# A planned one-core kernel: new port rules, prices and constants in the planner that orders its instructions

## The chip, the cores and the metric

The kernel runs on one core of a Trainium2 chip. The metric is device time of one execution in microseconds (us): the median over the runs. The names of the engines are those of the profile: PE multiplies matrices, DVE (VectorE) does elementwise work and reductions along a row, ACT (ScalarE) does copies, exponentials and gelu, POOL (GpSimd) does reductions across partitions here and nothing else, SP issues nearly all transfers. About 0.2% of the time (2.1 us) is what a measurement of this kernel can tell from no change.

## The reference

```python
def phi(x):
    proj = np.einsum('bhsd,df->bhsf', x, w_phi)
    proj = proj - np.max(np.abs(proj), axis=-1, keepdims=True)
    return np.concatenate([np.exp(proj), np.exp(-proj)], axis=-1)
q_p, k_p = (phi(q), phi(k))
kv = np.einsum('bhsf,bhsd->bhfd', k_p, v)
z = np.sum(k_p, axis=2)
num = np.einsum('bhsf,bhfd->bhsd', q_p, kv)
den = np.einsum('bhsf,bhf->bhs', q_p, z)[..., None] + 1e-06
attn = num / den                     # 8 batches, 8 heads, 576 tokens, 64
...
x = attn.transpose(0, 2, 1, 3).reshape(4608, 512)
h = x @ w_in                         # 512 x 2048
g = 0.5 * h * (1.0 + erf(h / sqrt(2)))
return g @ w_out                     # 2048 x 512
```

So eight batches of a linear attention with 128 features of both signs, and then a two-layer perceptron over all 4608 tokens. A token's row of x is whole only when all eight heads of its batch are done.

## The kernel before, in words

The attention goes batch by batch. For k: `pk` (PE, keys times features, in a PSUM tile "pp" that has one buffer and is shared with `pq`), `mx` (DVE, largest absolute value along the row, L435), the subtraction into `ek` or, for the rest of the keys, `er` (DVE, L371), two exponentials (ACT, L440), and `kv` (PE), copied out as `kvn`. The last two parts of a name such as `ek_1_1_1_1` say batch, half of the heads, pair in it and sign; only in batch 0 every second `pk` has another bank. For q: `pq` (PE), its copy `pc` (ACT, L365), `mb` (POOL, absolute maximum over the partitions, L501, one buffer), the subtraction `pc<-pc,mb` (DVE, L371), two exponentials `ef` (ACT), and `pn` (PE, one PSUM bank), copied out as `xo` (ACT) and stored to `x_d`. Of batches 0 and 1 the denominator is a row of `pn` (65 rows); from batch 2 on DVE makes `un` from `ef` (L530, L533) and POOL adds it over the partitions as `db` (L536). The quotients come from `d_d` by `dc` (L556, L557) and go to `r_d`.

The weights come as 32 pieces in 64-bit floats: `raw`, then `wt` by ACT (L386) and by four DVE steps (L387, L389 with one input, L391, L393 with two), then a high part (ACT, L365) and a low part (DVE, L371): `w_i` and `w_o`.

The perceptron goes in 18 blocks of 256 tokens. `tokens` (L588 on) loads `xr` and the quotients into `xh`, multiplies, and splits into `xh` and `xl` (all on DVE). `up` writes `ph` (24 matmuls for two columns of 128 features), then gelu into `gh` and `gl`, then `po`. Blocks 0 to 7 run beside the attention of batches 1 to 7 and the later weights. Blocks 8 to 17 use a product with seven instead of eight multiplications (`pa`, `pb`, with sums of weights `tw` that are stored as `t_d` and fetched when the attention's memory is given back).

Nothing of the order is written by hand. Every operation is given to `Plan.op` (L81) with its engine, a cost in us, and a rank. `Plan.order` (L109) is a list scheduler: for each engine it works out when each operation whose inputs are there could start (`start_of`, L128), takes the one that starts first, among equals the one of lowest rank, and moves that engine's clock. Between engines it adds `HOP` (L63); for a change of shape on PE `BEHIND` and `BEFORE` (L67, L68). `READS` (L70) is how long DVE is held at the start of a POOL reduction; `port` says which DVE operations are held. Ranks come from the constants at the end of the file: T0, LEAD, AT, HOLD and ATR for attention, T0, WR and WSPAN for weights, T0, T15 and T18 for the blocks, SUMSAT and SUMSEACH for the sums of weights. `emit` (L245) then issues all operations in the planned order, and each engine runs its own instructions in that order.

## Time and profile before

| what | value |
| --- | --- |
| median of 3 runs (lowest to highest) | 1070.29 us (1070.09 to 1070.43) |
| the profiled execution's own time | 1070.03 us |
| span in the trace, first to last instruction | 1068.3 us |
| mean granted clock of PE | 0.991 |
| busy: PE, DVE, ACT, POOL | 1037.0, 694.7, 625.8, 329.8 us |

Busy time is the sum of the stretches in which the engine works. "Idle before, releaser" in a row is the time that the engine stood still ahead of that instruction and what ended the wait. [...]

### The profile page before, as it was taken

How to read it: one execution, taken by the hardware profiler on the slowest of the kernel's cores; microseconds unless marked ns; L12 is line 12 of the kernel's file. 1: busy time of each engine (PE TensorE's matmuls, PEld its weight loads, DVE VectorE, ACT ScalarE, POOL GpSimd, SP SyncE). 2: the span in 40 equal slices, each digit the busy share in tenths (PEclk: the TensorE clock that was granted, in tenths of full speed). 3: DMA queues.
4: the chain of work that ended last, by engine and by line, in shares of the span. 5: the costliest groups of instructions: out<-in, count | busy, mean ns of one | idle time of the engine just before them, and what ended most of it. 6: DMA issues, size and time to landing. Idle time of an engine off the chain costs nothing.

```text
span 1068.3 us, 24224 instructions
## 1 busy us (share of the span) xinstructions
PE 1037.0 (97%) x9858; PEld 908.0 (85%) x9858; DVE 694.7 (65%) x1303; ACT 625.8 (59%) x1073; POOL 329.8 (31%) x116
## 2 busy tenths in 40 slices
...
GB/s 245 201 223 204 210 122 141 103 104 166 131 100 148 123 111 141 134 76 100 60 64 55 49 200 268 21 60 44 17 60 41 21 60 41 21 60 41 2 21 21
DMA packets 87392, 107.11 MB, mean 100 GB/s; under 512 B 25120, under 2 KB 68288, under 8 KB 87280
## 3 DMA queue, kind: packets, MB, share of 16 engines
...
q8 instruction: 77, 1.26, 0.5%
...
q10 hardware_dynamic: 144, 0.26, 0.1%
...
## 4 chain that ended last, share of the span: by engine, by line
PE 78%; DVE 10%; ACT 5%; issue 3%; DMA 3%; POOL 1%; SPq 0%; DVEq 0%; ACTq 0%; POOLq 0%
PE ph L330 32%; PE po L330 13%; PE pa L330 10%; PE pb L330 8%; PE pn L330 5%; PE kv L330 4%; PE pq L330 3%; PE pk L330 2%; DVE mx L435 1%; DVE ek L371 1%; DVE ts L371 1%; ACT ek L440 1%; DMA dc<-d_d 1%; POOL db L536 1%; DVE w_i L371 1%
## 5 line engine op out<-in xcount | busy, mean ns | idle before, releaser
L330 PE MATMUL ph<-xh,w_i 128*128 128x256 f32 x2304 | 411.9, 277 | 0.6 <-DVE gl L371 0.3
L330 PEld LDWEIGHTS ph<-xh,w_i 128*128 128x128 f32 x2304 | 355.1, 188 | 3.9 <-issue 2.4
L330 PE MATMUL ph<-xl,w_i 128*128 128x256 f32 x1152 | 318.3, 276 | 0.0
L536 POOL PARTITION_ALL_REDUCE db<-un x48 | 182.6, 3804 | 144.5 <-DVE un L533 133.0
L330 PEld LDWEIGHTS ph<-xl,w_i 128*128 128x128 f32 x1152 | 216.3, 188 | 0.3
L501 POOL PARTITION_ALL_REDUCE mb<-pc x64 | 149.5, 2337 | 148.5 <-ACT pc L365 106.0
L371 DVE TENSOR_TENSOR sg<-ga 128x256 f32<-128x256 f32 (+1 forms) x240 | 84.6, 375 | 149.8 <-ACT ga L710 149.0
L330 PE MATMUL po<-w_o,gh 128*128 128x512 f32 (+1 forms) x519 | 164.7, 400 | 0.0
L710 ACT ACTIVATE ga<-ph 128x512 f32<-128x512 f32 x80 | 47.8, 598 | 158.3 <-PE ph L330 156.6
L330 PEld LDWEIGHTS po<-w_o,gh 128*128 128x128 f32 x519 | 93.1, 188 | 28.5 <-issue 6.3
L330 PE MATMUL pa<-w_o,oh 128*128 128x256 f32 x640 | 112.8, 276 | 0.0
L330 PE MATMUL pn<-ef,kvn 128*64 128x288 f32 (+1 forms) x512 | 95.4, 419 | 6.5 <-ACT xo L365 6.4
L330 PE MATMUL po<-w_o,gl 128*128 128x512 f32 (+1 forms) x291 | 101.1, 367 | 0.1
L507 ACT ACTIVATE ef<-pc 128x576 f32<-128x576 f32 x128 | 81.8, 678 | 25.2 <-DVE pc L371 24.4
L330 PEld LDWEIGHTS pa<-w_o,oh 128*128 128x128 f32 x640 | 96.4, 188 | 0.0
L371 DVE TENSOR_TENSOR gl<-ph,gh 128x512 fp32r<-128x512 f32 x64 | 43.9, 688 | 73.9 <-ACT ph L633 70.2
L330 PE MATMUL pa<-w_o,ol 128*128 128x256 f32 x320 | 88.3, 276 | 0.0
L330 PE MATMUL pb<-tw,uh 128*128 128x256 f32 x480 | 85.6, 276 | 0.0
L440 ACT ACTIVATE ek<-ek 128x1024 f32<-128x1024 f32 x64 | 67.8, 1059 | 23.9 <-DVE ek L371 23.2
L530 DVE TENSOR_SCALAR un<-ef,kvn 128x288 f32<-128x288 f32 x96 | 53.3, 576 | 31.3 <-POOL db L536 23.5
L330 PEld LDWEIGHTS pb<-tw,uh 128*128 128x128 f32 x480 | 72.3, 188 | 0.0
L330 PEld LDWEIGHTS pn<-ef,kvn 128*64 128x64 f32 (+1 forms) x512 | 38.5, 136 | 38.0 <-ACT xo L365 14.0
...
## 6 DMA issues: line engine op xcount, KB each, us to landing
...
```

Source lines behind the costliest of these rows:

```text
L330: return tc.keep_in_program_order(nc.tensor.matmul(*a, **kw))
L371: op(eng, cost, lambda: e.tensor_tensor(out=dst(), in0=a(), in1=b(), op=o), r=r, w=w, **kw)
L435: op("dve", dve(256 * n, True), lambda: nc.vector.tensor_reduce(out=mx(), in_=xs(), axis=AX.X, op=ALU.max, apply_absolute_value=True), r=[ ...
L440: op("act", act(256 * n), lambda s=s: nc.scalar.activation(e[s](), e[1](), AF.Exp, scale=1.0 - 2.0 * s), r=[e[1]], w=[e[s]], table="exp", ...
L501: op("pool", 2.28, lambda mb=mb, pc=pc: nc.gpsimd.partition_all_reduce(mb(), pc(), P, bass_isa.ReduceOp.absmax), r=[pc], w=[mb], port="max ...
L507: op("act", act(2 * HS), lambda ef=ef, pc=pc, s=s: nc.scalar.activation(ef()[:, s], pc(), AF.Exp, scale=1.0 - 2.0 * s), r=[pc], w=[ef], ta ...
L530: op("dve", dve(HS, fast=True) + 0.06, lambda un=un, ef=ef, one=one, j=j: nc.vector.tensor_scalar(out=un()[:, j], in0=ef()[:, 0, j], scala ...
L536: op("pool", 3.8, lambda db=db, un=un: nc.gpsimd.partition_all_reduce(db(), un(), P, bass_isa.ReduceOp.add), r=[un], w=[db], port="add", * ...
L710: op("act", act(2 * TB, True) + 0.037, lambda ph=ph, ga=ga: nc.scalar.activation(ga(), ph(), AF.Gelu), r=[ph_all], w=[ga], table="gelu", a ...
```

## The change

Only the planner and its inputs change; each operation does what it did, and some `po` pairs that were emitted in two halves are emitted whole. Lines of the kernel after are 8 or 9 higher.

- `port` becomes a number: 1 for DVE operations with two inputs in SBUF, 2 for those with one (the memset, the first two steps of `wt`, the first step of `un`, the sum in `dc`, the cast to `xh`), 0 for those that read PSUM and for the reciprocal.
- A POOL reduction may start in the plan as soon as its input is there; its end is still counted from when DVE has finished (`port[0]`). The 0.45 us behind every POOL operation is gone.
- DVE is held in two windows: for `READS` from the start (port 1 and 2), and in a later window `WRITES` (port 2 alone).
- Leaving an `f` matmul (`ph`, `po`) for another shape is priced 0.09 us higher (`turn`), what PE waits for 0.07 us later (`PESLACK`), a quotient load at three times its bytes, the reductions at 2.14 and 3.59 us for 2.28 and 3.8.
- The constants were set anew.

```diff
-    READS = {"max": 1.12, "add": 2.38, "sum": 1.27}
+    READS = {"max": 1.15, "add": 2.45, "max main": 2.1, "add main": 4.43, "max rest": 1.05, "add rest": 2.15}
+    WRITES = {"max": (1.4, 2.02), "add": (2.75, 3.47), "max main": (2.3, 3.42), "add main": (4.6, 5.97), "max rest": (1.2, 1.83), "add rest": (2.4, 3.1)}
...
+    def turn(self, a, b):
+        return self.BEHIND[a] + self.BEFORE[b] + (0.09 if a == "f" and b != "d" else 0.0)
...
-        o.port = port if port is not None else eng == "dve"
+        o.port = port if port is not None else int(eng == "dve")
...
-            if o.eng == "pool" and o.port:
-                t = max(t, port[0])
...
-            if o.eng == "dve" and o.port and port[1] <= t < port[2]:
-                t = port[2]
+            if o.eng == "dve":
+                for a, z, least in port[1:]:
+                    if o.port >= least and a <= t < z:
+                        t = z
...
-                if best is None or key[1] < best[1]:
+                if best is None or key[1] < best[1] or key[1] == best[1] and e == "pool":
...
-            o.start, o.end = t, run(t, cost, o.duty) if o.eng == "pe" else t + cost
+            o.start = t
+            if o.eng == "pool" and o.port:
+                t = max(t, port[0])
+                a, z = self.WRITES[o.port]
+                port[1:] = [(t, t + self.READS[o.port], 1), (t + a, t + z, 2)]
+            o.end = run(t, cost, o.duty) if o.eng == "pe" else t + cost
...
-            clock[o.eng] = o.end + (0.45 if o.eng == "pool" else 0.0)
+            clock[o.eng] = o.end
...
-                    slot_free_at[b.tag][b.slot] = o.end + o.late + self.HOP[o.eng]
+                    slot_free_at[b.tag][b.slot] = o.end + o.late + self.HOP[o.eng] + (PESLACK if b.tag in self.banks else 0.0)
...
-            op("pool", 2.28, lambda mb=mb, pc=pc: nc.gpsimd.partition_all_reduce(
+            op("pool", 2.14, lambda mb=mb, pc=pc: nc.gpsimd.partition_all_reduce(
...
-                   r=[r_d[b][h]], w=[xh_all], kb=n * 1.024, rank=rank(0) - 8)
+                   r=[r_d[b][h]], w=[xh_all], kb=n * 3.0, rank=rank(0) - 8)
...
-WSPAN = 36.41
+WSPAN = 48.61
...
-LEAD = 217.42
+LEAD = 333.47
...
-T0 = 95.44
+T0 = 121.19
```

What DVE does at the very beginning: in the rows, `pc` is the query side of batch 0 and `mx`, `ek` its key side, `wt_i0_0` the first piece of the first weight. Before:

```order
L371 TENSOR_TENSOR pc_0_0_0_141<-pc_0_0_0_141,mb_0_0_0_145 128x576
L371 TENSOR_TENSOR er_0_1_166<-pk_0_r_156,mx_0_r_161 128x512
L435 TENSOR_REDUCE mx_0_0_0_196<-pk_0_0_0_173 128x8
L371 TENSOR_TENSOR pc_0_1_0_150<-pc_0_1_0_150,mb_0_1_0_170 128x576
L371 TENSOR_TENSOR ek_0_0_0_1_205<-pk_0_0_0_173,mx_0_0_0_196 128x1024
L435 TENSOR_REDUCE mx_0_0_1_210<-pk_0_0_1_185 128x8
L387 TENSOR_SCALAR wt_i0_0_194<-wt_i0_0_194 128x512
```

and after:

```order
L379 TENSOR_TENSOR pc_0_0_0_141<-pc_0_0_0_141,mb_0_0_0_145 128x576
L379 TENSOR_TENSOR er_0_1_168<-pk_0_r_156,mx_0_r_161 128x512
L395 TENSOR_SCALAR wt_i0_0_166<-wt_i0_0_166 128x512
L397 TENSOR_SCALAR wt_i0_0_166<-wt_i0_0_166 128x512
L399 SCALAR_TENSOR_TENSOR wt_i0_0_166<-raw_i0_0_128,wt_i0_0_166 128x512
L379 TENSOR_TENSOR pc_0_1_0_150<-pc_0_1_0_150,mb_0_1_0_170 128x576
L443 TENSOR_REDUCE mx_0_0_0_204<-pk_0_0_0_174 128x8
L443 TENSOR_REDUCE mx_0_0_1_211<-pk_0_0_1_191 128x8
L379 TENSOR_TENSOR ek_0_0_0_1_213<-pk_0_0_0_174,mx_0_0_0_204 128x1024
L379 TENSOR_TENSOR ek_0_0_1_1_215<-pk_0_0_1_191,mx_0_0_1_211 128x1024
```

Three steps of the first weight and one subtraction of queries now stand between `er_0_1` and the first `mx` of whole tiles, where before `mx_0_0_0` came directly.

DVE around the last `ek` of batch 1 (`ek_1_1_1_1`), whose matmuls `kv_1_1_1` stand shortly ahead of the first `ph` on PE; `wt_o4`, `wt_o5` are pieces of the second matrix, `xr_0` is the first block's tokens. Before:

```order
L435 TENSOR_REDUCE mx_1_1_1_959<-pk_1_1_1_903 128x8
L371 TENSOR_TENSOR pc_1_0_0_878<-pc_1_0_0_878,mb_1_0_0_899 128x576
L371 TENSOR_TENSOR w_i1_1_957<-wt_i1_1_838,w_i1_1_957 128x512
L371 TENSOR_TENSOR w_i2_1_963<-wt_i2_1_848,w_i2_1_963 128x512
L371 TENSOR_TENSOR ek_1_1_1_1_979<-pk_1_1_1_903,mx_1_1_1_959 128x1024
L387 TENSOR_SCALAR wt_i3_1_984<-wt_i3_1_984 128x512
L371 TENSOR_TENSOR xr_0_540<-xr_0_540,xh_0_859 128x1024
L389 TENSOR_SCALAR wt_i3_1_984<-wt_i3_1_984 128x512
```

and after:

```order
L379 TENSOR_TENSOR pc_1_1_0_911<-pc_1_1_0_911,mb_1_1_0_934 128x576
L395 TENSOR_SCALAR wt_o4_936<-wt_o4_936 128x512
L395 TENSOR_SCALAR wt_o5_945<-wt_o5_945 128x512
L397 TENSOR_SCALAR wt_o4_936<-wt_o4_936 128x512
L397 TENSOR_SCALAR wt_o5_945<-wt_o5_945 128x512
L399 SCALAR_TENSOR_TENSOR wt_o4_936<-raw_o4_769,wt_o4_936 128x512
L443 TENSOR_REDUCE mx_1_1_1_977<-pk_1_1_1_950 128x8
L401 SCALAR_TENSOR_TENSOR wt_o4_936<-raw_o4_769,wt_o4_936 128x512
L399 SCALAR_TENSOR_TENSOR wt_o5_945<-raw_o5_852,wt_o5_945 128x512
L379 TENSOR_TENSOR xr_0_481<-xr_0_481,xh_0_781 128x1024
L379 TENSOR_TENSOR w_o4_1030<-wt_o4_936,w_o4_1030 128x512
L379 TENSOR_TENSOR ek_1_1_1_1_1038<-pk_1_1_1_950,mx_1_1_1_977 128x1024
```

The same `ek` now stands behind the token product `xr_0` and behind pieces of `w_o4` and `w_o5` that stood behind it; its row on DVE is 103, and was 87.

PE from the last `kv` of batch 1 to the first matmul of block 0 (`ph_0_0`); the rows of `kv_1_1_1` between are left out. Before:

```order
L330 MATMUL pn_0_3_1_1_999<-ef_0_3_1_856,kvn_0_1_1_524 65x288 x2
L330 MATMUL pk_2_r_1009<-wst_114,kr_2_389 128x128 x4
L330 MATMUL kv_1_1_1_1026<-vt_1_1_844,er_1_0_557 64x65 x2
...
L330 MATMUL kv_1_1_1_1026<-vt_1_1_844,ek_1_1_1_1_979 64x65 x2
L330 MATMUL pn_1_0_0_0_1076<-ef_1_0_0_970,kvn_1_0_0_772 65x288 x2
L330 MATMUL pn_1_0_0_1_1094<-ef_1_0_0_970,kvn_1_0_0_772 65x288 x2
L330 MATMUL pq_1_1_1_1107<-qt_1_1_1_895,wst_114 128x288 x2
L330 MATMUL pq_1_2_0_1126<-qt_1_2_0_1002,wst_114 128x288 x2
L330 MATMUL pn_1_0_1_0_1133<-ef_1_0_1_1019,kvn_1_0_0_772 65x288 x2
L330 MATMUL pk_2_0_0_1144<-wst_114,kt_2_0_713 128x128 x8
L330 MATMUL pn_1_0_1_1_1165<-ef_1_0_1_1019,kvn_1_0_0_772 65x288 x2
L330 MATMUL ph_0_0_1172<-xh_0_859,w_i0_0_287 128x256
```

and after:

```order
L338 MATMUL pn_1_0_0_0_1033<-ef_1_0_0_887,kvn_1_0_0_765 65x288 x2
L338 MATMUL pk_2_r_1052<-wst_114,kr_2_417 128x128 x4
L338 MATMUL pn_1_0_0_1_1060<-ef_1_0_0_887,kvn_1_0_0_765 65x288 x2
L338 MATMUL kv_1_1_1_1072<-vt_1_1_874,er_1_0_556 64x65 x2
...
L338 MATMUL kv_1_1_1_1072<-vt_1_1_874,ek_1_1_1_1_1038 64x65 x2
L338 MATMUL pn_1_0_1_0_1130<-ef_1_0_1_1024,kvn_1_0_0_765 65x288 x2
L338 MATMUL pk_2_0_0_1148<-wst_114,kt_2_0_763 128x128 x8
L338 MATMUL ph_0_0_1163<-xh_0_781,w_i0_0_280 128x256
```

`pq_1_1_1`, `pq_1_2_0` and `pn_1_0_1_1` no longer stand ahead of `ph_0_0`; they come behind it. `kv_1_1_1` has two `pn` of batch 1 ahead of it that stood behind.

## Rows read from the trace of the kernel before

**Rows 1.** Windows over four stretches of the span. Columns: stretch, its length, then busy us (with the count of instructions) of PE, PE's weight loads, DVE, ACT, POOL, then the granted clock, the DMA engines' share and GB/s.

```profile
0.00:94.70 94.70, 75.42 (x948) 50.01 (x949) 74.49 (x109) 67.19 (x115) 31.74 (x16) 0.91 0.73 222
94.70:190.00 95.30, 91.67 (x863) 72.32 (x861) 90.23 (x142) 78.48 (x124) 27.68 (x10) 1.00 0.53 159
190.00:640.00 450.00, 447.39 (x4359) 364.70 (x4360) 301.46 (x464) 311.01 (x467) 270.36 (x91) 1.00 0.36 109
640.00:1068.00 428.00, 422.55 (x3692) 420.97 (x3691) 228.48 (x590) 169.09 (x368) 0.00 (x0) 1.00 0.17 51
```

**Rows 2.** Waits of PE in the first 94.7 us. Columns: what waited, for whom, us in total, times, longest.

```profile
PE pn L330 <- ACT xo L365: 3.9, 6, 1.6
PE pq L330 <- DVE ek L371: 3.2, 2, 1.8
PE pq L330 <- ACT pc L365: 2.7, 3, 1.2
PE pk L330 <- ACT pc L365: 1.9, 3, 1.0
```

**Rows 3.** The same from 94.7 to 190 us.

```profile
PE pn L330 <- ACT xo L365: 1.0, 1, 1.0
PE pk_r L330 <- ACT pc L365: 0.8, 1, 0.8
PE pk L330 <- DVE er L371: 0.7, 1, 0.7
...
PE ph L330 <- DVE w_i L371: 0.3, 1, 0.3
```

**Rows 4.** The same from 190 us to the end.

```profile
PE pn L330 <- ACT xo L365: 1.5, 2, 1.3
PE pk L330 <- ACT pc L365: 0.8, 1, 0.8
```

**Rows 5.** The timeline of DVE, four places from the beginning to the last split of block 0's tokens; columns: start, length, engine, line, operation and tiles, count, and in brackets the idle time before and its releaser. From the start of one row to the start of the next is what an instruction costs there.

```profile
15.41 1.23 DVE L435 TENSOR_REDUCE mx<-pk 128x8 f32<-128x1024 f32 x1 [2.22 <-PE pk L330]
16.55 0.75 DVE L371 TENSOR_TENSOR pc<-pc,mb 128x576 f32<-128x576 f32 x1
17.22 1.21 DVE L371 TENSOR_TENSOR ek<-pk,mx 128x1024 f32<-128x1024 f32 x1
...
19.48 0.41 DVE L387 TENSOR_SCALAR wt_i<-wt_i 128x512 f32<-128x512 f32 x1
19.82 1.21 DVE L371 TENSOR_TENSOR ek<-pk,mx 128x1024 f32<-128x1024 f32 x1
20.95 1.26 DVE L389 TENSOR_SCALAR wt_i<-wt_i 128x512 uint32<-128x512 uint32 x1
22.13 1.10 DVE L387 TENSOR_SCALAR wt_i<-wt_i 128x512 f32<-128x512 f32 x1
23.15 0.67 DVE L391 SCALAR_TENSOR_TENSOR wt_i<-raw_i,wt_i 128x512 uint32<-128x512 uint32 x1
23.75 0.41 DVE L389 TENSOR_SCALAR wt_i<-wt_i 128x512 uint32<-128x512 uint32 x1
...
78.14 1.21 DVE L371 TENSOR_TENSOR ek<-pk,mx 128x1024 f32<-128x1024 f32 x1
...
89.91 1.21 DVE L371 TENSOR_TENSOR xl<-xr,xh 128x1024 fp32r<-128x1024 f32 x1
```

**Rows 6.** The timeline of PE ahead of the first `ph`. Columns as before.

```profile
79.41 0.76 PE L330 MATMUL pq<-qt,wst 64*128 64x288 f32 x4 [1.83 <-DVE ek L371]
...
81.77 1.23 PE L330 MATMUL pk_r<-wst,kr 64*128 64x128 f32 x8
82.93 1.13 PE L330 MATMUL kv<-vt,er 128*64 128x65 f32 x16
...
85.89 1.19 PE L330 MATMUL pn<-ef,kvn 128*65 128x288 f32 x4
...
90.62 0.76 PE L330 MATMUL pq<-qt,wst 64*128 64x288 f32 x4 [1.19 <-ACT pc L365]
91.30 1.19 PE L330 MATMUL pn<-ef,kvn 128*65 128x288 f32 x4
92.42 1.16 PE L330 MATMUL pk<-wst,kt 64*128 64x128 f32 x16
...
94.70 0.50 PE L330 MATMUL ph<-xh,w_i 128*128 128x256 f32 x1
```

**Rows 7.** The timeline of PE in the middle, where it leaves `ph` for another shape.

```profile
441.87 0.28 PE L330 MATMUL ph<-xl,w_i 128*128 128x256 f32 x1
441.99 0.28 PE L330 MATMUL ph<-xh,w_i 128*128 128x256 f32 x1
442.19 1.19 PE L330 MATMUL pn<-ef,kvn 128*64 128x288 f32 x8
```

**Rows 8.** The timeline of SP where the sums of weights are fetched for block 8.

```profile
632.55 4.24 SPq L691 DMA_DIRECT2D tw<-t_d  x8
```

**Rows 9.** The first matmuls that use them: one tile's instructions, their count, shortest, median and longest ns, and first and last start.

```profile
L330 PE MATMUL pb<-tw,uh x480: 276/276/280, 661.2 to 1062.2; 128*128 128x256 f32 x160
```

**Rows 10.** The timeline of POOL, one of its reductions at the beginning.

```profile
20.63 2.32 POOL L501 PARTITION_ALL_REDUCE mb<-pc  x1 [5.73 <-ACT pc L365]
```

**Rows 11.** Groups of POOL in the first 94.7 us. Columns: line, engine, operation, tiles, count, then busy us and mean ns of one, then idle us before them and what ended most of it.

```profile
L501 POOL PARTITION_ALL_REDUCE mb<-pc x12 | 31.6, 2629 | 61.1 <-ACT pc L365 50.7 <-DVE pc L371 5.1 <-ACT ek L440 3.5
```

More of the change, by code (lines that the diff above doesn't have):

```diff
@@ L125, in order @@
         gelus, left_at, dma, dge = [0], [0.0], [0.0], [0.9]
-        port = [0.0, 0.0, 0.0]
+        port = [0.0]
         def start_of(o):
             t = max(clock[o.eng], o.ready)
-            if o.eng == "pool" and o.port:
-                t = max(t, port[0])
             if o.table == "exp" and table[0] == "gelu" and gelus[0] % (2 * STICK):
@@ L209, in order @@
                 if self.SHAPE[last[0]] != self.SHAPE[o.kind]:
-                    cost += self.BEHIND[last[0]] + self.BEFORE[o.kind]
+                    cost += self.turn(last[0], o.kind)
                 last[0] = o.kind
-            o.start, o.end = t, run(t, cost, o.duty) if o.eng == "pe" else t + cost
+            o.start = t
[4 more added lines that the diff above has]
+            o.end = run(t, cost, o.duty) if o.eng == "pe" else t + cost
             if o.nbytes:
@@ L219, in order @@
                 left_at[0] = o.end
-            clock[o.eng] = o.end + (0.45 if o.eng == "pool" else 0.0)
+            clock[o.eng] = o.end
             if o.eng == "dve" and o.port:
                 port[0] = o.end
-            if o.eng == "pool" and o.port:
-                port[1:] = [o.start, o.start + self.READS[o.port]]
             for b in o.bufs:
@@ L234, in order @@
                 if b.left == 0 and b.tag is not None:
-                    slot_free_at[b.tag][b.slot] = o.end + o.late + self.HOP[o.eng]
+                    slot_free_at[b.tag][b.slot] = o.end + o.late + self.HOP[o.eng] + (PESLACK if b.tag in self.banks else 0.0)
             for u in o.users:
                 u.wait -= 1
-                u.ready = max(u.ready, o.end + o.late + (self.HOP if u.eng != o.eng else self.SAME)[o.eng] + (POOLSLACK if o.eng == "pool" else 0.0))
+                u.ready = max(u.ready, o.end + o.late + (self.HOP if u.eng != o.eng else self.SAME)[o.eng] + (POOLSLACK if o.eng == "pool" else 0.0) + (PESLACK if u.eng == "pe" and o.eng != "pe" else 0.0))
                 if u.wait == 0:
@@ L350, in fused_kernel @@
     idle = sb["gl"]([P, 512], F32, "idle")
-    op("dve", dve(512, fast=True), lambda: nc.vector.memset(idle(), 0.0), w=[idle], rank=-500.0)
+    op("dve", dve(512, fast=True), lambda: nc.vector.memset(idle(), 0.0), w=[idle], rank=-500.0, port=2)
     op("act", act(1), lambda: nc.scalar.activation(idle()[:, :1], idle()[:, :1], AF.Exp), r=[idle], w=[idle], table="exp", rank=-500.0)
@@ L530, in q_pair @@
                         op("dve", dve(HS, fast=True) + 0.06, lambda un=un, ef=ef, one=one, j=j: nc.vector.tensor_scalar(
-                            out=un()[:, j], in0=ef()[:, 0, j], scalar1=one(), scalar2=None, op0=ALU.mult), r=[ef, kvn], w=[un], **k())
+                            out=un()[:, j], in0=ef()[:, 0, j], scalar1=one(), scalar2=None, op0=ALU.mult), r=[ef, kvn], w=[un], port=2, **k())
                     else:
@@ L555, in quotients @@
         op("sp", 0.06, lambda: nc.sync.dma_start(out=dc(), in_=spread(d)), r=[d], w=[dc], kb=9, rank=next(rank))
[L556 to L557 removed]
+        op("dve", 0.09, lambda: nc.vector.tensor_scalar(out=dc(), in0=dc(), scalar1=SHIFT, scalar2=None, op0=ALU.add), r=[dc], w=[dc], port=2, rank=next(rank))
+        op("dve", 0.19, lambda: nc.vector.reciprocal(out=dc(), in_=dc()), r=[dc], w=[dc], port=0, rank=next(rank))
         op("sp", 0.06, lambda: nc.sync.dma_start(out=spread(r), in_=dc()), r=[dc], w=[r], kb=9, rank=next(rank))
```

34 lines of the change are left out of this document (17 added, 17 removed).

## The prediction

> **What bounds the kernel now.** I read the windows first, cut where the work changes: to the first `ph`, to where the weights are done, to where attention is done, and blocks 8 to 17. In each the reader should compare PE's busy time with the length [rows 1]. PE stands still for 19.3 us of the first 94.7, for 3.6 of the next 95.3, for 2.6 of the next 450 and for 5.5 of the last 428. So PE bounds the kernel, and an order can win only the idle time, the clock below 1.00 at the beginning, and changes of shape on PE. Then I read PE's waits by stretch. In the first they are spread over `pn` waiting for the copy `xo`, `pq` waiting for `ek` or a copy, `pk` waiting for a copy [rows 2], none of them a load. After 94.7 us the named waits are 1.0, 0.8, 0.7 and 0.3 [rows 3], after 190 us the two that are left are 1.5 and 0.8 [rows 4]. The last 428 us have no POOL work, and the order there is practically the old one; the 5.5 us are mostly the additions and the store behind the last matmul, which stay. DVE is busy for 74.5 of the first 94.7 us and for 90.2 of the next 95.3 [rows 1]: it is what PE waits for at the beginning, directly or through ACT, and it is what the change reorders.
>
> **The change part by part.** No instruction is added or taken away but for a few `po` halves that are emitted whole (their matmuls cover the same columns). So the sum has four terms, all against the profiled execution's 1070.03 us, 0.26 under the median.
>
> First, the start of block 0. In the old trace `ek_1_1_1_1` runs on DVE from 78.14 and ends at 79.35 [rows 5]; PE is waiting for it there, since `pq` needs the bank that it reads [rows 6]. In the new order 16 more DVE instructions stand ahead of it. At the start-to-start prices of rows 5 (one-input step 0.34, two-input step 0.60, `pc` 0.67, `mx`, `ek` and `xr` 1.13) they are five steps of `w_i3_1` for 2.47, two `pc` for 1.34, `xr_0` for 1.13, and eight steps of `w_o4` and `w_o5` for 3.74: 8.7 us in all. Against this stands the hole of 2.22 us at 15.41 [rows 5]: there the new order has three steps of `wt_i0` and a `pc`, so I take it as filled. And DVE loses a little to POOL as it goes: from 79.35 to the end of `xl_0` at 91.12 are 11.8 us for 11.0 us of work at the same prices, 0.07 per us, which makes 0.6 over 8.7. So `ek_1_1_1_1` ends at 79.35 + 8.7 - 2.2 + 0.6 = 86.5. It would be 84.4 if 2.1 more of DVE's small holes close, and 88.7 if the filled hole only moves (the last step of `wt_i0` is followed by steps that wait for ACT).
>
> From that end to the first matmul of `kv` on its results, two exponentials and two `pn` or `pk` pass: about 3.0 us, where the old trace has 3.6 to the start of `kv` (79.35 to 82.93) with a `pq`, a `pn` and a `pk_r` between [rows 6]. So `kv_1_1_1` starts at about 89.5, takes 2.96 (82.93 to 85.89), and a `pn` of 1.1 and a `pk` of 1.1 follow [rows 6]. `ph_0_0` comes at 94.7, as now. But the work that PE has done by then is less: `pq_1_1_1` and `pq_1_2_0` at 0.69 each and one `pn` of 1.1 now stand behind it, 2.5 us that come back between the blocks. Term: +2.5, from +0.4 (`ek` at 84.4) to +4.7 (`ek` at 88.7). That ACT can give the two exponentials at once is assumed; a queue of weight copies ahead of them on ACT is inside the upper end.
>
> The other edges of `ph_0_0`: `xl_0` has 66.5 us of DVE work ahead of and in it, where it had 65.2, and its overhead would be 25.9 less the 2.2, so it ends near 90.6, and `er_2_1`, which `pk_2_0_0` waits for, now stands behind `xl_0` and two weight steps, at some 92.5. A `pk` of 1.1 then leads to 93.6: not later than the 94.7 above, but close.
>
> Second, the waits from 94.7 to 190 us, 3.6 now. In this stretch DVE is nearly full, and the new order puts less in front of what PE needs: by the same prices `gl_0_6` has 127.0 us of DVE work up to it and not 130.1, and of eight `mb` and a `db` that POOL does from `xl_0` to block 1's first `gl`, six and one are left, the others falling later where DVE has slack. Three us less work and two all-reduces are more than the 2.8 named in rows 3, but the two `pq` and the `pn` of the first term land in the same stretch. I take -2.4; all of it would be -3.6, none 0.
>
> Third, the waits from 190 to 640, 2.6 now, where rows 4 are single events. The planner now lets PE's inputs be 0.07 later and leaves `f` less readily, and each of them is late by little; but new single events can come. I take -1.8, between -2.6 and 0.
>
> Fourth, changes of shape on PE. In the old trace the step from `ph` to `pn` costs 0.20 start to start, where two matmuls of `ph` in a row cost 0.12 [rows 7]: 0.08 more. From `ph_0_0` to the first `ph` of block 8 I count 234 such changes in the new order and 221 in the old. Thirteen more at 0.08 to 0.09 are +1.2 (+0.5 if only the six that change between blocks and attention count).
>
> Costed at nothing: the fetch of `tw`. It begins at 632.55 and the first `pb` is at 661.2 [rows 8, 9]; PE's work from the last `pn` to the first `pb` falls from 40.6 to 37.9 us, so some 24 us of cover become 21. Without that cover the 2.7 would be paid. The quotient loads at three times their price are the same transfers; in blocks 12 and later one of them stands behind two stores on SP, and is needed a block later. The clock: it is 0.91 on average ahead of 94.7 and 1.00 after [rows 1]; PE is as busy in the new beginning, and I leave it.
>
> Sum: +2.5 - 2.4 - 1.8 + 1.2 = -0.5, so 1069.5 by the profiled execution, and 1069.8 for the median, which lies 0.26 higher.
>
> One mechanism decides whether the new port rules can give anything: does POOL hold DVE for the whole reduction? The reduction at 20.63 lasts 2.32 [rows 10], to 22.95. A one-input step that stands beside it starts at 20.95 and its successor at 22.13 [rows 5]: one step finishes 0.7 us before the reduction does, and the next is done only at 23.23. So DVE gets a step in the middle, as the new `READS` and `WRITES` have it. [...]
>
> **The rivals.** Faster: DVE's holes ahead of `ek_1_1_1_1` close further and it ends at 84.4, and all named waits behind 94.7 go. Then +0.4 - 3.6 - 2.6 + 1.2 = -4.6, and the median 1065.7. For it: the 11.7 us of waits for copies and `ek` [rows 2] are of the kind that a better priced order removes, and PE's spare work (`pq`, `pn`) is now behind `ph_0_0` and can fill. Against: rows 5 show DVE with hardly a hole between 16 and 24 us, so there is little to close.
>
> Slower: `ek_1_1_1_1` is the one instruction, its place behind `xr_0` and `w_o4` (the second pair of orders above) is the mechanism, and 8.7 us of work its price. If the hole at 15.41 isn't won, `ek` ends at 88.7, `ph_0_0` starts at 96.9, and PE has nothing ready while it waits: +4.7. With half of the later waits kept (-1.8 for the two terms of -4.2, after new ones) and +1.2: +4.1, so a median of 1074.4. It decides from an end of `ek` of about 87.5 on. For it: DVE is the fuller engine there. Against: PE has `kv_1_1_0` and `pn_1_0_0_0` to do before it comes to what waits for `ek`.
>
> [...]
>
> That it doesn't do what it says: the terms cancel, or the new order, planned with prices nearer to the trace, moves waits about without changing their sum. This is the forecast's own range.
>
> **How the numbers follow.** Forecast 0.37, faster rival 0.37, slower rival 0.22, lock 0.04. The forecast's own range is 1067 to 1072.4, of which a little reaches over the bound of 0.2% (2.1 us: faster is below 1068.2, slower above 1072.4). Faster 0.38, the same 0.36, slower 0.26. The range that holds the time 8 times in 10 is 1063.5 to 1074.5: below, the faster rival and 2 us more (0.09 of the 75.4 us that PE works before 94.7 at 0.91 [rows 1] are 6.8 us, a third of which could come back with a denser beginning); above, the slower rival.
>
> **What would show it.** Right: `ek_1_1_1_1` ends at 86 to 87, `ph_0_0` starts at 94 to 96; DVE has no hole before the first whole `mx`; PE's idle time from 94.7 to 190 is about 1.2 us and from 190 to 640 about 0.8; the first `pb` does not wait for `tw`. Wrong: `ph_0_0` later than 97 or earlier than 92; a new PE wait of over 1 us behind 190; PE's busy time (1037 now) moving by more than 2 us, which would mean clock or shape changes that the terms do not hold; a wait of `pk` for `er_2_1`.

## The result and the profile after

The kernel after takes 1077.13 us (median of 4 runs, 1074.36 to 1077.88), the kernel before 1070.36 (4 runs): a ratio of 1.0059, 95% interval 1.0039 to 1.0078. It is slower by 6.8 us by the medians and 6.3 by the ratio, outside the forecast's range. The profiled execution took 1077.82 us with a span of 1075.9; busy are PE 1043.8, DVE 683.9, ACT 617.2 and POOL 321.2 us. DVE and POOL are busy for 10.8 and 8.6 us less than before, with the same number of instructions (1303 and 116): a reduction `mb` takes 2.29 us in the mean for 2.34, a `db` 3.69 for 3.80. That the port rules did this, which they were made for, no run tests apart. PE is busy for 6.8 us more and idle for 0.8 us more (32.1 for 31.3 of the span).

The windows of after answer to [rows 1], with the same columns; the fourth ends at 1075, and the last row is the stretch up to the first `ph` as it now lies.

```profile
0.00:94.70 94.70, 71.30 (x823) 46.95 (x824) 70.43 (x103) 59.41 (x102) 26.87 (x15) 0.87 0.69 212
94.70:190.00 95.30, 94.08 (x929) 74.59 (x928) 82.54 (x136) 80.31 (x126) 19.34 (x8) 1.00 0.53 164
190.00:640.00 450.00, 448.18 (x4360) 361.32 (x4359) 300.19 (x475) 306.55 (x471) 274.95 (x93) 1.00 0.34 105
640.00:1075.00 435.00, 430.25 (x3746) 428.17 (x3744) 230.73 (x591) 170.96 (x370) 0.00 (x0) 1.00 0.18 56
...
0.00:101.93 101.93, 78.43 (x937) 51.92 (x937) 77.63 (x117) 66.14 (x113) 26.87 (x15) 0.88 0.66 201
```

Behind 94.7 us PE stands still for less than before: 1.2 us and 1.8 us where it was 3.6 and 2.6. The loss is ahead of `ph_0_0`, which starts at 101.93 and not at 94.70, with 23.5 us of idle time ahead of it (101.93 less 78.43; before 19.3) and a lower granted clock: 0.88 up to there, before 0.91 up to 94.70; behind 94.7 us it is 1.00 in every row of both. PE's waits of after, in the first 100 us and, below the dots, from 190 to 640 us, answer to [rows 2] and [rows 4]:

```profile
PE pn L338 <- ACT xo L373: 4.9, 8, 1.8
PE pk L338 <- DVE ek L379: 3.6, 1, 3.6
PE pq L338 <- issue: 3.3, 1, 3.3
PE kv L338 <- ACT kvn L373: 3.0, 2, 2.8
PE pq L338 <- ACT pc L373: 2.7, 2, 1.9
...
PE po L338 <- ACT gh L640: 0.7, 1, 0.7
PE po L338 <- DVE gl L379: 0.5, 1, 0.5
PE pn L338 <- ACT ef L515: 0.4, 1, 0.4
```

Three single waits of about 3 us stand out. `pk` for `ek` and `kv` for `kvn` are new; `pq` for an issue has grown (in before its longest was 1.5). DVE's timeline answers to [rows 5]: the place of the old hole, two waits for ACT, the wait for POOL, and the key chain of batch 1 from `ek_1_1_0_1` (the `ek` at 85.16) to `ek_1_1_1_1` (the `ek` at 94.07).

```profile
14.05 1.23 DVE L395 TENSOR_SCALAR wt_i<-wt_i 128x512 f32<-128x512 f32 x1
15.32 0.99 DVE L397 TENSOR_SCALAR wt_i<-wt_i 128x512 uint32<-128x512 uint32 x1
...
43.20 0.69 DVE L379 TENSOR_TENSOR w_i<-wt_i,w_i 128x512 fp32r<-128x512 f32 x1 [3.07 <-ACT w_i L373]
...
61.79 0.69 DVE L379 TENSOR_TENSOR w_o<-wt_o,w_o 128x512 fp32r<-128x512 f32 x1 [2.14 <-ACT w_o L373]
...
82.15 0.76 DVE L379 TENSOR_TENSOR pc<-pc,mb 128x576 f32<-128x576 f32 x1 [2.04 <-POOL mb L509]
...
85.16 1.22 DVE L379 TENSOR_TENSOR ek<-pk,mx 128x1024 f32<-128x1024 f32 x1
...
94.07 1.23 DVE L379 TENSOR_TENSOR ek<-pk,mx 128x1024 f32<-128x1024 f32 x1 [0.54 <-PE kv L338]
```

`ek_1_1_1_1` ends at 95.30, 15.9 us later than before. What DVE waits for up to that end, in after (first three rows) and, below the dots, in before up to its 79.35:

```profile
DVE w_i L379 <- ACT w_i L373: 3.9, 3, 3.1
DVE w_o L379 <- ACT w_o L373: 3.2, 3, 2.1
DVE pc L379 <- POOL mb L509: 2.0, 1, 2.0
...
DVE mx L435 <- PE pk L330: 3.6, 2, 2.2
DVE w_o L371 <- ACT w_o L365: 2.4, 1, 2.4
DVE w_i L371 <- ACT w_i L365: 1.4, 1, 1.4
```

PE's timeline answers to [rows 6]:

```profile
29.38 0.69 PE L338 MATMUL kv<-vt,er 128*64 128x65 f32 x16 [2.78 <-ACT kvn L373]
...
86.53 2.08 PE L338 MATMUL pk<-wst,kt 64*128 64x128 f32 x16 [3.65 <-DVE ek L379]
88.53 2.18 PE L338 MATMUL pn<-ef,kvn 128*65 128x288 f32 x4
90.64 1.14 PE L338 MATMUL kv<-vt,er 128*64 128x65 f32 x16
91.56 2.57 PE L338 MATMUL kv<-vt,ek 128*64 128x65 f32 x64
94.07 1.19 PE L338 MATMUL pn<-ef,kvn 128*65 128x288 f32 x4
...
96.00 1.19 PE L338 MATMUL pn<-ef,kvn 128*65 128x288 f32 x4
97.11 0.69 PE L338 MATMUL kv<-vt,er 128*64 128x65 f32 x16
...
99.69 1.19 PE L338 MATMUL pn<-ef,kvn 128*65 128x288 f32 x4
100.84 1.16 PE L338 MATMUL pk<-wst,kt 64*128 64x128 f32 x16
101.93 0.39 PE L338 MATMUL ph<-xh,w_i 128*128 128x256 f32 x1
```

From 86.53 on no wait of PE is named up to `ph_0_0`, but the `pk` and `pn` at 86.53 and 88.53 last nearly twice as long as those at 100.84 and 96.00. From 86.53 to 94.07 PE takes 7.5 us for a `pk`, a `pn` and a `kv` that cost 4.8 from start to start further down (1.09, 1.11 and 2.58).

Orders differ, so start times of one operation in two kernels don't compare directly. Below, **PE's loss** at an operation is its start less all the PE work that its kernel's order has ahead of it, each matmul at its start-to-start price where the granted clock is 1.00, changes of shape included. It is my count from orders and rows.

| PE's loss, us | before | after | difference |
| --- | --- | --- | --- |
| at `ph_0_0` | 27.0 | 36.5 | +9.5 |
| at block 1's first `po` | 30.2 | 36.4 | +6.2 |
| at `ph_8_0` | 32.7 | 39.3 | +6.6 |
| at `ph_17_0` | 32.7 | 39.6 | +6.9 |

With 0.8 us more work (985.0 for 984.2 up to `ph_17_0`) that is 7.7 of the 7.8 us between the profiled executions. So in the profiled executions 9.5 us are lost ahead of `ph_0_0`, 3.3 come back by block 1's first `po`, and the rest runs as before.

Such a difference between two executions holds the order's share and also what changes from one execution to the next. The head below is the order up to `ph_0_0`. Three executions with the head of before start `ph_0_0` at 94.7, 95.0 and 98.1, and three with that of after at 101.9, 101.8 and 98.8. So one execution's `ph_0_0` is good to about 3 us, and small differences in it prove nothing; medians do better.

### The profile page after: what moved, and what is told of

The parts are those of the page before. It is cut to its first block, busy times and chain, and to the rows that moved or that the text cites. A ratio compares the mean times of both kernels' runs of the same rounds, so it can differ in the third digit from the quotient of the medians.

```text
span 1075.9 us, 24158 instructions
## 1 busy us (share of the span) xinstructions
PE 1043.8 (97%) x9851; PEld 911.0 (85%) x9851; DVE 683.9 (64%) x1303; ACT 617.2 (57%) x1067; POOL 321.2 (30%) x116
## 4 chain that ended last, share of the span: by engine, by line
PE 54%; DVE 0%; issue 0%; ACT 0%
PE ph L338 26%; PE pa L338 10%; PE pb L338 7%; PE po L338 6%; PE pn L338 2%; PE kv L338 1%; PE pq L338 1%; PE pk L338 0%; DVE ob L379 0%; DVE gl L379 0%; PE pk_r L338 0%; ACT ob L373 0%
## 5 line engine op out<-in xcount | busy, mean ns | idle before, releaser
L544 POOL PARTITION_ALL_REDUCE db<-un x48 | 177.3, 3693 | 114.6 <-DVE un L541 107.8
L509 POOL PARTITION_ALL_REDUCE mb<-pc x64 | 146.4, 2287 | 194.4 <-ACT pc L373 166.7
L515 ACT ACTIVATE ef<-pc 128x576 f32<-128x576 f32 x128 | 82.5, 680 | 30.3 <-DVE pc L379 29.6
L379 DVE TENSOR_TENSOR pc<-pc,mb 128x576 f32<-128x576 f32 x64 | 57.9, 905 | 37.5 <-POOL mb L509 37.5
L448 ACT ACTIVATE ek<-ek 128x1024 f32<-128x1024 f32 x64 | 67.6, 1058 | 18.2 <-DVE ek L379 17.5
L338 PEld LDWEIGHTS pn<-ef,kvn 128*64 128x64 f32 (+1 forms) x512 | 39.5, 138 | 37.8 <-ACT xo L373 11.2
```

Of the source, the lines that this page charges most:

```text
L338: return tc.keep_in_program_order(nc.tensor.matmul(*a, **kw))
L379: op(eng, cost, lambda: e.tensor_tensor(out=dst(), in0=a(), in1=b(), op=o), r=r, w=w, **kw)
L448: op("act", act(256 * n), lambda s=s: nc.scalar.activation(e[s](), e[1](), AF.Exp, scale=1.0 - 2.0 * s), r=[e[1]], w=[e[s]], table="exp", ...
L509: op("pool", 2.14, lambda mb=mb, pc=pc: nc.gpsimd.partition_all_reduce(mb(), pc(), P, bass_isa.ReduceOp.absmax), r=[pc], w=[mb], port="max ...
L515: op("act", act(2 * HS), lambda ef=ef, pc=pc, s=s: nc.scalar.activation(ef()[:, s], pc(), AF.Exp, scale=1.0 - 2.0 * s), r=[pc], w=[ef], ta ...
L544: op("pool", 3.59, lambda db=db, un=un: nc.gpsimd.partition_all_reduce(db(), un(), P, bass_isa.ReduceOp.add), r=[un], w=[db], port="add", ...
```

## The experiments

Planned orders are written out as a list of operations, which the scheduler takes in place of its own choice:

```diff
+            if given:
+                o = self.ops[given.pop(0)]
+                best = (None, start_of(o), o)
-            for e, lst in cand.items():
+            for e, lst in ({} if best else cand).items():
```

**Halves of the order, the planner going on by itself.** old_head_new_tail:

```diff
+GIVEN = before's order up to ph_0_0 (391 operations); the planner of after plans the rest
```

> The order of all engines is that of the kernel before up to ph_0_0, then the new planner goes on. Theory HEAD (all of the loss is made ahead of ph_0_0, where DVE reaches ek_1_1_1_1 16 us later; behind it the new order wins about 3 us): ph_0_0 at 94.5 to 95.5, PE standing still under 1.5 us from there to 190, median 1066 to 1069. Rival TAIL (the new order behind ph_0_0 costs, by turns and new waits): median 1072 or more. Rival NOISE (the new kernel's runs are only less steady): about 1070 with a spread of over 2 us.

Measured 1081.3 us, 1.0087 (1.0054 to 1.0120): HEAD's range was missed and TAIL's met. But behind 190 us the planner made another rest than after's, with new waits: PE's loss goes from 30.4 at `ph_0_0` to 44.1. So the median tests neither, since a planner that starts from another state plans something else. `ph_0_0` starts at 98.1 where HEAD had 95.5 at most, although the order of PE, DVE, ACT and POOL up to there is before's. DVE reaches the end of `ek_1_1_1_1` at 79.24, as in before, and then stands still for a load of quotients:

```profile
81.66 1.23 DVE L383 TENSOR_TENSOR xr<-xr,xh 128x1024 f32<-128x1024 f32 x1 [2.08 <-DMA xh<-r_d]
```

In before this wait isn't there, though its loads were issued only 0.3 us earlier. new_head_old_tail:

```diff
+GIVEN = after's order up to ph_0_0 (393 operations); the planner of before plans the rest
```

> The order of the new kernel up to ph_0_0, then the old planner. HEAD: ph_0_0 at 100 to 103, PE waits again some 3 us from there to 190, median 1077 to 1082, not below the new kernel's. TAIL: median 1070 to 1073.

Measured 1079.53, 1.0082 (1.0056 to 1.0107). The median lies where HEAD put it, `ph_0_0` at 98.8 lies earlier than HEAD's 100, and the rest was planned anew here too.

**Rules and constants apart.** new_rules_old_constants (old_rules_new_constants is the reverse):

```diff
-WSPAN = 48.61
+WSPAN = 36.41
...
-LEAD = 333.47
+LEAD = 217.42
...
-T0 = 121.19
+T0 = 95.44
```

> The new planner with the old constants at the end of the file. Its head comes out much like the new kernel's (ek_1_1_1_1 is DVE's instruction 104, where it is 103 and was 87). HEAD, with the rules as its cause: ph_0_0 at 99 or later and a median of 1074 or more. Rival CONSTANTS (the new constants spoil the head): 1069 to 1072.

> The old planner with the new constants. ek_1_1_1_1 is DVE's instruction 94 with 58.3 us of work up to it by the planner's costs (54.4 before, 63.1 new), and three more PE operations stand ahead of ph_0_0 than before. HEAD with the rules as its cause: the wait for ek is at most half as late as in the new kernel, median 1069 to 1074, below new_rules_old_constants. CONSTANTS: 1075 or more.

Measured 1098.86, 1.0259 (1.0233 to 1.0286), with `ph_0_0` at 96.8, and 1089.25, 1.0166 (1.0142 to 1.0190). The first median lies in the range that blamed the rules, though `ph_0_0` came earlier than its 99, and the second lies in the range that blamed the constants. Both are far worse than either kernel: each set of constants fits its own rules alone, and these two runs give neither part of the change a price of its own.

**Grafts of exact orders.** graft_old_head and graft_new_head:

```diff
+GIVEN = before's order up to ph_0_0, then what is left of after's order, unchanged
```

> Every engine's order is written out: up to ph_0_0 that of the kernel before, and from there exactly the new kernel's (less what the old head has already done). In old_head_new_tail the planner made another rest, so it did not test this. HEAD: ph_0_0 at 94.5 to 98, no more than 1.5 us of further PE loss up to 190, median 1066 to 1069. Rival FIT (a rest is only good behind the head it was planned with, since DVE, ACT and the banks stand elsewhere at the seam): 1073 or more, with a new PE wait of over 1 us behind 100 us.

```diff
+GIVEN = after's order up to ph_0_0, then what is left of before's order, unchanged
```

> The new order up to ph_0_0 and behind it exactly the old one (five PE operations stand elsewhere for the banks' sake). HEAD: median 1077 to 1081, PE's waits of some 3 us from 95 to 190 are back. FIT: over 1081.

In graft_new_head and in the four cuts below, an operation that can't be planned yet is passed over until it can, so a few stand elsewhere than written.

graft_old_head: 1072.10, 1.0024 (1.0012 to 1.0035). The old head takes away 3.7 of the 6.3 us by the ratios, and the intervals of this graft and of after don't touch. HEAD's range (1066 to 1069) and FIT's (1073 or more) were both missed. Its windows up to `ph_0_0` and from there to 190, and its PE waits in the second:

```profile
0.00:95.00 95.00, 73.45 (x949) 48.40 (x949) 75.25 (x110) 66.81 (x115) 32.13 (x16) 0.96 0.72 222
95.00:190.00 95.00, 91.39 (x858) 73.98 (x856) 80.90 (x136) 77.36 (x119) 19.11 (x8) 1.00 0.52 161
```

```profile
PE po L342 <- DVE gl L383: 1.3, 2, 0.8
PE pn L342 <- ACT xo L377: 1.1, 2, 0.7
PE kv L342 <- ACT ek L452: 0.8, 1, 0.8
```

`ph_0_0` is back at 95.0 (loss 27.2), but PE stands still for 3.6 us up to 190, exactly as before (3.6) and not as in after (1.2), though the order there is after's. So behind the old head that order saves nothing (loss 33.9 at `ph_17_0`, before 32.7). The likely reading is that in after PE came late and its inputs were ready; that the joint of the two orders ate a saving isn't excluded. graft_new_head: 1081.86, 1.0112 (1.0098 to 1.0126), over 1081 as FIT had it, with `ph_0_0` at 101.8, and the loss grows on to 46.0. Its first window:

```profile
0.00:101.83 101.83, 75.58 (x940) 49.19 (x941) 78.94 (x118) 66.70 (x114) 27.29 (x15) 0.92 0.69 205
```

Under the same head before's rest does 5 to 6 us worse than after's (1.0112 for 1.0059): head and rest fit each other, and a joint has a price of its own.

**Single waits of the new head.** new_pc_later takes away DVE's wait for POOL; new_act_copies, new_xo_first and new_old_start each put right one queue, and new_three_moves all three together:

```diff
 DVE (new_pc_later)
-pc_1_0_1
 w_i2_1, mx_1_1_0, w_i3_1, ek_1_1_0_1
+pc_1_0_1
-pc_1_1_0
 wt_o4, wt_o5 ..., xr_0
+pc_1_1_0
```

```diff
 ACT (new_act_copies)
+kvn_0_0_0, pc_0_3_0
 wt_i2_0, wt_i3_0
-kvn_0_0_0, pc_0_3_0
```

```diff
 ACT (new_xo_first)
+xo_0_3_1_0
 wt_o4
-xo_0_3_1_0
 PE
+pn_0_3_1_1
 pk_1_1_1
-pn_0_3_1_1
```

```diff
 DVE (new_old_start)
+mx_0_0_0, pc_0_1_0, ek_0_0_0_1, mx_0_0_1
 wt_i0_0 (its first step)
+ek_0_0_1_1
-pc_0_1_0, mx_0_0_0, mx_0_0_1, ek_0_0_0_1, ek_0_0_1_1
```

> The new kernel's written order with two DVE instructions moved: the subtraction pc_1_0_1, ahead of which DVE stands still for 2.0 us because POOL's reduction took 3.8, goes behind ek_1_1_0_1, and pc_1_1_0 behind xr_0. Nothing else moves. Theory POOLWAIT (that wait, by way of PE's wait of 3.6 us for ek_1_1_0_1 and the low clock behind it, makes a third of the head's loss): PE's longest wait ahead of ph_0_0 falls to 2.3 or less, ph_0_0 comes 1.5 to 4 us earlier, median 1073 to 1075.5. Rival ELSEWHERE (the ends of the other waits, ACT's casts above all, are just as late): within 1 us of the new kernel's 1077.

> The new kernel's written order; on ACT alone the copies kvn_0_0_0 and pc_0_3_0 go ahead of the two steps wt_i2_0 and wt_i3_0, which wait for DVE (rows of the new kernel: PE stands still 2.8 us for that kvn). Theory QUEUE (the head is lost by copies out of PSUM that stand in ACT's queue behind weight steps): the PE wait for kvn falls under 1, ph_0_0 1 to 2.5 us earlier than with no move, median 1075 to 1076. Rival DVEBOUND (DVE's own chain sets ph_0_0 whatever PE does in between): the wait goes, but ph_0_0 and the median (1076.5 to 1077.5) stay.

> The new kernel's written order; on ACT xo_0_3_1_0 goes ahead of wt_o4, and on PE pn_0_3_1_1 ahead of pk_1_1_1, so that PE works 1.1 us in the wait of 3.6 for ek_1_1_0_1. QUEUE: PE's longest wait there falls to 2.6 or less, less low clock behind it, median 1074.5 to 1076. DVEBOUND: 1076.5 to 1077.5.

> The new kernel's written order; on DVE the first eight instructions of the keys stand as before (mx, pc, ek, mx ahead of the steps of wt_i0). QUEUE: the wait of pq for the bank (3.3 us) falls to 1.6 or less, median 1075 to 1076.5. DVEBOUND: the steps of wt_i0 are only done later, so what was won is lost by ph_0_0: 1076.5 to 1077.5, or slower.

> The three moves together. QUEUE: ph_0_0 at 94 to 97, median 1070 to 1073. DVEBOUND: ph_0_0 not before 98, median 1075 or more.

| run | us | ratio (95%) | `ph_0_0` at | the wait aimed at | what is long instead |
| --- | --- | --- | --- | --- | --- |
| new_pc_later | 1076.66 | 1.0061 (1.0049 to 1.0073) | 100.2 | DVE for POOL 2.0, now none named | `pk` for `ek` 3.6 stays |
| new_act_copies | 1077.68 | 1.0065 (1.0054 to 1.0076) | 100.2 | `kv` for `kvn` 2.8, now 0.6 | `pk` for `ek` 5.3, `pk_r` 2.7 |
| new_xo_first | 1077.15 | 1.0060 (1.0049 to 1.0072) | 100.1 | `pk` for `ek` 3.6, now 0.3 | `pn` for `xo` 8.4 |
| new_old_start | 1079.29 | 1.0081 (1.0068 to 1.0094) | 101.0 | `pq` for issue 3.3, now 1.5 | `kv` for `kvn` 4.7 |
| new_three_moves | 1077.16 | 1.0064 (1.0050 to 1.0077) | 99.6 | `pk` for `ek` gone, `pq` for issue 1.6, `kv` for `kvn` 2.5 stays | `pn` for `xo` 8.9 |

Waits of `pn` for `xo` are sums (4.9 in after). Each run meets the rival that expected no gain (new_act_copies lies 0.2 us above that rival's range). In four of the runs the wait aimed at goes or shrinks, and the time comes back at another wait or the longest one stays; in new_three_moves one of the three stays as well. No time is gained. The waits of PE in the first 100 us of new_xo_first:

```profile
PE pn L345 <- ACT xo L380: 8.4, 9, 2.8
PE pq L345 <- issue: 3.3, 1, 3.3
PE kv L345 <- ACT kvn L380: 2.9, 2, 2.7
```

**Less weight work in the head.** Ahead of `er_2_1`, DVE's and ACT's steps for the weights are put back by one weight, or by two:

```diff
 DVE, ACT (new_weights_one_later; two weights in new_weights_two_later)
-the weights' steps in their places, the first weight's first
+each place takes the step of one weight earlier, the first weight's places stay empty,
+the last weight's steps come behind er_2_1
```

> The new kernel's written order with the weight stream ahead of er_2_1 put back by one weight on DVE and ACT: each weight step stands where the same step of the next weight stood, and the last weight's steps follow behind er_2_1. All else keeps its place. Up to ek_1_1_1_1 DVE has 3 us less work. Theory WEIGHTS (the new head is late since DVE and ACT do weights there that nothing needs yet): ph_0_0 2 to 4 us earlier than in the runs with the new head (99.6 to 102), median 1073 to 1075.5. Rival DVEFLOW (DVE is the bound from the beginning to about 190 us, so what ph_0_0 wins PE loses again waiting for gl or w_i): ph_0_0 earlier by the same, but more PE waits behind it, median 1076 to 1078. Rival TANGLE (the three queues wait for each other about as long wherever the weights stand): ph_0_0 within 1 us of 100, median 1076 to 1078.

> The same with two weights: 6 us less DVE work up to ek_1_1_1_1, less than in the kernel before up to ek_1_0_0_1. WEIGHTS: ph_0_0 4 to 7 us earlier, median 1071 to 1074. DVEFLOW: ph_0_0 at 94 to 97, PE waits from there to 190 rise by 3 us or more, median 1076 to 1079. TANGLE: ph_0_0 within 2 us of 100.

Measured 1100.65, 1.0281 (1.0267 to 1.0295), and 1093.28, 1.0205 (1.0191 to 1.0219). DVE has 3 and 6 us less work ahead of `ek_1_1_1_1`, yet that ends at 113.7 and 100.2. DVE's longest waits ahead of `ph_0_0`, of the first and of the second:

```profile
DVE wt_i L402 <- ACT wt_i L401: 18.7, 5, 5.5
```

```profile
DVE pc L386 <- POOL mb L516: 13.3, 5, 5.3
```

In the first DVE stands at a weight step whose first step ACT does late, in the second at a `pc` whose reduction POOL does late. All the numbers expected were missed: `ph_0_0` comes at 121.7 and 108.7. The new waits (18.7 and 13.3 us) are far larger than the work put back, so these runs don't tell what less work alone would give. They show that how the places in the queues stand to each other can outweigh it.

**PE's spare work in the order before.** old_ph_earlier lets block 0 begin earlier in the kernel before:

```diff
 DVE
 er_2_1
+xl_0
 pc_1_1_1
+mx_2_0_0
 PE
+ph_0_0 (its first 12 matmuls)
 pq_1_2_0
```

> The kernel before with its written order and three moves: on DVE xl_0 directly behind er_2_1 and mx_2_0_0 behind pc_1_1_1, on PE the first twelve matmuls of ph_0_0 ahead of pq_1_2_0, which waits 1.2 us for a copy. If PE's waits there can be filled: PE's waits from 88 to 100 fall by 1.2 us or more and the median is 1068 to 1069.3. DVEFLOW: the same time as before within 0.1%, since DVE's work is the same.

Measured 1071.45, 1.0007 (0.9998 to 1.0016): no difference, as DVEFLOW had it. `ph_0_0` starts at 89.1 (loss 25.2, before 27.0), and at the end of block 0's `po` the loss is 30.3, before 29.7. The gain is gone at once: the wait of 1.2 us is filled, and others come (up to 104 us `pn` for `xo` 2.0 where it was 0.8, `po` for `gl` 0.7).

**Cutting the head.** Four grafts join the two orders earlier: at `kv_0_1_0` (about 34 us), and at `kv_1_0_0` (51 us in before, 58 in after).

```diff
+GIVEN = before's order up to kv_0_1_0 (kv_1_0_0), then what is left of after's      # cut_old_to_...
+GIVEN = after's order up to kv_0_1_0 (kv_1_0_0), then what is left of before's      # cut_new_to_...
```

> The order of before up to the first matmul of kv_0_1_0 (about 34 us), then exactly what is left of the order of after. FIRST (the beginning makes the loss: PE had lost 14.0 us there and 17 to 18 in after, and what comes later follows from it): PE's loss stays at 14 to 15 by 40 us and the median is near the 1072.1 of the graft at ph_0_0, 1071 to 1073. LAST (the piece behind it makes the loss, and takes up any gain from the beginning): 1076 to 1078, with the wait of pk for ek_1_1_0_1 as long or longer. FIT (no piece is good or bad by itself, each joint costs): above 1078.

> The order of before up to the first matmul of kv_1_0_0 (about 51 us there), then exactly what is left of the order of after. FIRST: 1071 to 1073, as the run with the earlier cut. LAST: 1076 to 1078, if the loss is made from 60 us to ph_0_0. FIT: above 1078.

> The order of after up to the first matmul of kv_0_1_0, then exactly what is left of the order of before. FIRST: PE's loss of 17 to 18 by 40 us stays, so before's 1070.3 and 3 to 4: 1073 to 1075. LAST: the beginning is taken up by slack behind it, 1070 to 1072. FIT: above 1076.

> The order of after up to the first matmul of kv_1_0_0 (about 58 us there), then exactly what is left of the order of before. FIRST: 1073 to 1076. LAST: 1070 to 1072.5. FIT: above 1076.

| order | us | ratio (95%) | PE's loss at 36 us | `ek_1_1_1_1` ends | `ph_0_0` at |
| --- | --- | --- | --- | --- | --- |
| old to `kv_0_1_0`, then new | 1078.51 | 1.0071 (1.0058 to 1.0084) | 14.8 | 93.8 | 100.4 |
| old to `kv_1_0_0`, then new | 1078.53 | 1.0075 (1.0063 to 1.0088) | 14.7 | 96.3 | 102.9 |
| old to `ph_0_0`, then new | 1072.10 | 1.0024 (1.0012 to 1.0035) | 14.7 | 79.3 | 95.0 |
| new to `kv_0_1_0`, then old | 1074.40 | 1.0037 (1.0024 to 1.0051) | 17.7 | 83.4 | 102.2 |
| new to `kv_1_0_0`, then old | 1076.99 | 1.0057 (1.0044 to 1.0069) | 17.4 | 86.2 | 101.5 |
| new throughout | 1077.13 | 1.0059 (1.0039 to 1.0078) | 17.4 | 95.3 | 101.9 |

FIT's ranges are met by the first two and the fifth (above 1078 and above 1076), FIRST's by the fourth (1073 to 1075), LAST's by none. In the first two rows the joint itself shows. PE stands still for over 4 us directly behind it; the first row below is of cut_old_to_kv010, the second of cut_old_to_kv100:

```profile
39.08 2.18 PE L343 MATMUL pn<-ef,kvn 128*65 128x288 f32 x4 [4.18 <-ACT xo L378]
...
57.08 2.18 PE L343 MATMUL pn<-ef,kvn 128*65 128x288 f32 x4 [4.85 <-ACT xo L378]
```

The longest such wait in after is 1.8. So PE's lead at 36 us (14.7 for 17.4; in the first row the long wait is already under way there) is lost at the joint, and these rows don't show what the later piece costs by itself. The fourth row has the new beginning alone and costs 4 us, but its profile is of the slowest of its five runs (1077.93; the others take 1074.16 to 1075.43), in which DVE waits 2.0 us for a load of quotients at `xr`. So its 102.2 doesn't belong to its median. What is left is weaker than either theory: either piece of the new head, joined to before's, costs 4 to 8 us, and how much of that is the piece and how much the joint stays open. DVE's waits in the first 104 us of cut_old_to_kv100 show the same joint from DVE's side:

```profile
DVE w_o L384 <- ACT w_o L378: 7.9, 4, 4.5
DVE mx L448 <- PE pk L343: 3.1, 2, 2.0
DVE pc L384 <- POOL mb L514: 2.0, 1, 2.0
```

DVE stands for 7.9 us at `w_o` steps for ACT, where after has 3.2 up to the end of `ek_1_1_1_1`.

## Why the prediction was wrong

**The first term failed, and with it the forecast**, in its time and in its path. It put the end of `ek_1_1_1_1` at 86.5, with bounds of 84.4 and 88.7; it came at 95.30. The work was counted rightly: 8.7 us more on DVE ahead of it. The step that failed is "- 2.2 (the hole) + 0.6": it let DVE's time beyond that work fall by 1.6 us, and that time grew by 7.2 (15.9 less 8.7). Of the 7.2, 5.2 are idle time of DVE (it is busy for 71.0 of the 95.3 us, in before for 60.3 of 79.35), the rest instructions that lasted longer. The hole was filled, as forecast. But two of the steps that fill it, at 14.05 and 15.32, stand beside a reduction (13.71 to 16.03) and cost 1.27 and 1.02 from start to start where the sum used 0.34: 1.6 of the 2.2 us are lost again. Waits for ACT's casts, for which the sum had no term, were there before (3.8 us) and grew to 7.1; that for `pk` fell from 3.6 to 1.9; the wait of 2.04 for POOL is new; 0.95 us is a later first instruction, which comes with either order (the first `mx_r` starts at 11.2 to 12.6 with the head of before). A term of work moved past other work was taken for the whole, while every instruction that gets new neighbours can also wait for another queue. The true upper bound needed these waits, which the diff of the order doesn't show.

The size differs between executions. With the head of after `ek_1_1_1_1` ends at 95.30, 93.87 (graft_new_head) and 92.15 (new_head_old_tail), so the time beyond the work grew by 4.1 to 7.2; with that of before it ends at 79.2 to 79.4 in three executions. All three of after's lie above the upper bound.

The path failed too. It led through a wait of PE for `ek_1_1_1_1`, and in after PE doesn't wait for it. The long wait is for the `ek` before it, `ek_1_1_0_1` (`pk` at 86.53, 3.65). That one ends 17.5 us later (86.38) than in before, where its row is

```profile
67.71 1.22 DVE L371 TENSOR_TENSOR ek<-pk,mx 128x1024 f32<-128x1024 f32 x1
```

It has 17 more instructions and, by my count at the same prices, 8.8 us more work ahead of it, and the forecast had no term for it. Behind it PE works on without a named wait, 2.8 us longer than the `pk`, `pn` and `kv` from 86.53 to 94.07 cost further down, and comes to `kv_1_1_1` 1.8 us after `ek_1_1_1_1` has ended, when its inputs are there. So from that end to `ph_0_0` 6.6 us pass where the forecast had 8.2, which returned part of the error.

**The second term** was right in size (forecast -2.4, -3.3 by PE's loss up to block 1's `po`; idle time 1.2 as in the list) but its cause is not borne out: graft_old_head has the order of after there and stands still for 3.6 us, so the size may be luck. **The third** (-1.8) gave nothing: the idle time fell from 2.6 to 1.8, and PE's loss grew by 2.9 from block 1 to `ph_8_0`, before by 2.5. **The fourth** (+1.2): PE's work grew by 0.8 by my count. **The fetch of `tw`** cost nothing, as forecast: no wait of PE is named behind 640 us.

**The clock**, which was left as it was, fell from 0.91 to 0.87 in the first 94.7 us, and PE's busy time grew by 6.8 us, more than the 2 us that the prediction named as a sign of being wrong. Read alone, this would be the whole loss. The grafts speak against it: before and graft_old_head have 0.91 and 0.96 there, 75.4 and 73.45 us of busy time, and `ph_0_0` at 94.7 and 95.0; graft_new_head has 0.92 and 75.58 us for 78.43 in after, and `ph_0_0` at 101.8 for 101.9. Where PE was quicker, it waited longer: in graft_new_head the `pk` ahead of the long wait takes 1.16 us and the wait is 5.26, in after 1.83 and 3.65, and the next `pk` starts at 85.73 and 86.53. Of the four runs of after the one with a mean clock of 0.987 took 1077.82 us, and one with 0.992 took 1077.88. The 2.8 us above stand in a stretch, 86.53 to 94.07, whose granted clock was 0.59. That a denser beginning gives clock back, which the lower end of the forecast's range assumed, was the author's estimate and isn't shown: up to `ph_0_0` PE is idle for 19.3 us in before at 0.91, and for 21.6 in graft_old_head at 0.96. What share the low clock has in single runs (the other runs of the new head begin `ph_0_0` at 98.8 to 101.8) wasn't tested apart.

**The rivals.** The slower one had sign and engine right and was too cheap (1074.4): it priced `xr_0` and `w_o4` ahead of `ek_1_1_1_1`, while the long wait of PE was for the `ek` before it. The chance of 0.04 (lock) was for a DVE that is kept out for the whole of each reduction. No run shows that: the steps at 14.05 and 15.32 start inside a reduction (13.71 to 16.03) and last 1.23 and 0.99 us, where one alone takes 0.41 [rows 5]; the first of them ends at 15.28, inside it. They are stretched, not kept out.

**What is shown and what is open.** Shown: over half of the loss goes with the order up to `ph_0_0` (graft_old_head 1.0024, after 1.0059); behind the old head the new rest is not better than the old one; no single one of the four waits moved gives the time back, nor do three together. Open: which part of the head makes the loss, since each joint costs something itself, and whether less weight work there would help. That DVE, ACT and POOL, each in its fixed order, pass the delay on to one another fits all these runs, but is an argument from them: no run breaks that chain and gets the time back. Which of the new rules or constants led the planner there is open as well, since each fits only its partner.
